# A fused gated pair of attention blocks on one core: the order of a step's matmuls written out for zero, one and two side blocks

## The chip, the core and the metric

The kernel runs on one NeuronCore of a Trainium2 chip. The metric is device time in microseconds (us) from launch to end, the median of several runs. The engines named below: TensorE (PE in the profile) multiplies and writes to PSUM; VectorE (DVE) and ScalarE (ACT) read PSUM; GpSimd (POOL) works on SBUF; SyncE (SP) issues the DMAs.

## The reference

```python
H = 32; Dh = 20                       # x: (1, 2048, 640); two weight sets, A and B
g = sigmoid((x * gate_w).sum(-1, keepdims=True))
for z in (A, B):
    q, k, v = split(x @ wqkv_z)       # per head: (2048, 20)
    p = softmax(q @ k.T * Dh ** -0.5)
    y_z = (p @ v per head, joined) @ wo_z
out = g * y_A + (1 - g) * y_B
```

Both attentions read the same x; 64 heads of dimension 20 in all, each with a 2048 x 2048 score matrix.

## The kernel before

**Tiling.** The 64 heads are taken in 16 groups of four (`g`), each group's 2048 queries in four blocks of 512 (`qb`), and each block's keys in eight pieces of 256 (`i`): 16 x 4 x 8 = 512 steps, numbered `G`. The four heads sit as two pairs (`pair`); within a pair head `j = 0` uses rows 0 to 63 of TensorE's array and `j = 1` rows 64 to 127, so two matmuls of different `j` can run side by side, and two of the same `j` come one after the other.

**What a step does on TensorE.** Eight score matmuls (`scores`, L640, 64 x 128 by 64 x 512; "e" below): each fills one PSUM bank, from which ScalarE writes an exponential (L643) into a `pt` tile. Eight matmuls for row maxima (`max_mm`, L577; "m" below): scores again, with queries and keys exchanged, 14 steps ahead of their use, each for a quarter of the 2048 keys; VectorE reduces the bank to a maximum (L588). A quarter is `ch`; the tuple `ORDER` says in which order the quarters of a unit come. For quarter 0 of `j = 0` (and of both `j` in the first group of heads) TensorE takes differences of keys of two quarters (`KD`), ScalarE writes their relu into `rl` (L581), and quarter 1's instruction on VectorE (L585) adds its own bank to it; `rl` has two buffers. Two blocks of four matmuls (`values`, L658; "V" below) weigh the previous step's exponentials with V into the one bank `acc`. They use four column strips of the array, 128 rows deep, in float32.

**Side blocks.** Projections of the next group's Q, K and V (`project_chunk`, `project_v`) and the output products (`out_tiles`, `last_tiles`) wait in the list `fill` with a first step and a due step. `slot(G)` emits one block of the one that is due first: mostly 15 full-array matmuls into one bank (L378; "X" below), copied out by ScalarE or added by VectorE. `behind(G)` says whether what is due needs more than one block in each step.

**Banks.** One of the eight PSUM banks is `acc`; the other seven serve e, m, X and the small products in turn. `take()` gives the bank that a planner's clock holds free for longest. Every engine works through its own instructions in the program's order, so a matmul whose bank is not free stops all behind it on TensorE.

**The order in a step.** The loop at the end of the program runs `q` over 0 to 7. At each `q` it emits one e, then m's that `max_step` hands out at even `q` (`j` in the order 1, 0), at `q` in `VPOS = (0, 5)` a V, and at `BLOCKS = (3, 6)` an X: at 3 if there is work, at 6 only if `behind`. So a step with one block reads, on TensorE: e m V e m e m e m X e m e m V e m e m. After the second V of the step that ends a block of queries, `take_acc` has ScalarE copy `acc` out (L743); the next V writes `acc` anew and has to wait for that copy. `advance()` after each e moves the side generators (DMAs, small vector work), eight times a step, and `todo` and `out_tasks` follow at the fourth e.

Of the kernel before, what the change touches and what calls it, by code (L numbers as in the profile page):

```python
# [31 lines left out]
NS = 8  # L32
STEPS = 2 * NG * NQ * NS
LEAD = 15
# [1 line left out]
XE = 7  # L36
QKS = 2.0 ** -12
PARTS = (0, 176, 344, 512)
BLOCKS = (3, 6)
RS = 2.0 ** 13  # L40
OB = 3
OWAIT = 20
SUM0, SUM1 = -8, 1.9
VPOS = (0, 5)
RAMP = 1.5
WEAVE = (4, 4, 3, 2)
VSTART = 14
# [3 lines left out]
T_EXP, T_MAX, T_BACK = 0.478, 0.6, 0.15  # L51
REST = 3
PRODUCT = "product"
ORDER = (0, 2, 1, 3)
LOW = -3.0e38
MS = 2.0 ** 15

# [2 lines left out]
def kernel(  # L60
# [210 lines left out]
    side = []  # L271
# [17 lines left out]
    def product():  # L289

        if parked:
            gen = parked.pop(0)
            goes = step_on(gen)
            if goes is not None:
                (side if goes else parked).append(gen)
# [256 lines left out]
    def unit_of(u):  # L552
        gq, i = divmod(u, NS)
        g, qb = divmod(gq, NQ)
        return g, qb, i
# [97 lines left out]
    def values(G, kk):  # L653
        g, qb, i = unit_of(G)
        tick_block(T_VALUES, weighed.pop((G, kk)))
        kt = 2 * i + kk
        for h in range(GH):
            nc.tensor.matmul(acc[32 * h:32 * h + VW, :], V[(g // 2) % 2][:, kt, (g % 2) * GH + h, :],  # L658
                             ptiles.pop((G, kk, h)), start=(kt == 0), stop=(kt == NT - 1))
# [296 lines left out]
    for g in range(2 * NG):  # L956
        b = g * NQ * NS
        n = g + 1
# [82 lines left out]
    def spread_of(u):  # L1041
        g, qb, i = unit_of(u)
        return {(g, qb)} if g == 0 else {(g, 0), (g, 1)}

    def max_step(G):

        ms = []
        if maxima and maxima[0][0] < G + LEAD and spread_of(maxima[0][0]) <= spread_done:
            debt[0] += 1.0 if maxima[0][0] - G >= LEAD - 1 else RAMP
            n, debt[0] = int(debt[0]), debt[0] % 1  # L1050
            for u, ch in maxima[:n]:
                ms += [lambda u=u, ch=ch, j=j: max_mm(u, ch, (j,)) for j in (1, 0)]
                if u % NS == NS - 1 and ch == ORDER[3]:
                    finishing.append(unit_of(u)[:2])
            del maxima[:n]
        return ms

    finishing = []

# [7 lines left out]
    for G in range(STEPS + 1):  # L1067
        g, qb, i = unit_of(G)
        now[0] = G
        while G < STEPS and ((g, qb) not in ready or (G and not valued(G - 1))):  # L1070
            for f in max_step(G):
                f()
            finish_step()
            advance()
            product()
            slot(G)
        for q in range(8):
            if q % 2 == 0:
                ms = max_step(G)
            n = (len(ms) + 1) // 2 if q % 2 == 0 else len(ms)  # L1080
            if G < STEPS:
                scores(G, q // 4, q // 2 % 2, (q % 2,))
            for f in ms[:n]:
                f()
            ms = ms[n:]
            if not ms:
                finish_step()
            for k in range(2):
                if q == VPOS[k]:
                    product()  # L1090
                    if G:
                        values(G - 1, k)
                        if G % NS == 0 and k == 1:
                            if G < STEPS:
                                side.append(take_acc(*unit_of(G - 1)[:2]))
                                advance()
            advance()
            if q == BLOCKS[0] or (q == BLOCKS[1] and behind(G)):
                slot(G)
            if q == 3:  # L1100
                for f in todo.pop(G, []):
                    f()
                out_tasks(G)
    end_o = take_last()
    while side or parked or fill or current or outs or last:
        advance()
# [32 lines left out]
```

## Time and profile before

| | us |
|---|---|
| median of 3 runs | 2934.09 |
| lowest, highest | 2932.76, 2935.25 |
| the profiled execution's own time | 2937.35 |
| its span, first to last instruction | 2935.5 |

The profile is of one execution. Busy times of TensorE include time in which matmuls overlap, and their ends are modelled; starts are what is read below.

### The profile page before, as it was taken

What the parts mean: (1) busy time and instruction counts of PE and PEld (TensorE: products, weight loads), DVE (VectorE), ACT (ScalarE), POOL (GpSimd) and SP (SyncE); (2) the same over time, 40 slices, a digit from 0 to 9 for tenths busy, and PEclk for the clock granted to TensorE, in tenths of its full rate; (3) what the DMA queues carried; (4) which work ended last, traced back from release to release, by engine and by line L of the source; (5) the groups of instructions that cost most, each with busy time, mean ns of one, the idle gap of its engine ahead of it and who ended that gap; (6) DMA issues with size and microseconds to landing.
All of it is one profiled execution on the core that took longest, in us unless ns stands there. A gap on an engine that the chain in (4) does not pass through costs nothing.

```text
span 2935.5 us, 63883 instructions
## 1 busy us (share of the span) xinstructions
PE 2843.9 (97%) x23474; PEld 984.7 (34%) x23474; DVE 2452.1 (84%) x4645; ACT 2539.1 (86%) x5221; POOL 655.0 (22%) x1078
## 2 busy tenths in 40 slices
PE   5999999999999999999999999999999999999998
PEld 2433323343223323234233333334433333332222
DVE  5688898878988898887988888887788888989983
ACT  2389999989988999888998989998899999988886
POOL 3221212221121212222521121222112233120010
PEclk8899999999999999999999999999999999999999
DMA  3110101101021010211112111120111212122222
GB/s 115 34 42 17 24 21 24 33 6 35 11 47 26 15 32 12 51 22 34 33 31 55 25 42 31 30 53 14 40 33 33 62 26 71 49 65 73 63 60 72
DMA packets 179839, 114.59 MB, mean 39 GB/s; under 512 B 115084, under 2 KB 153508, under 8 KB 179524
## 3 DMA queue, kind: packets, MB, share of 16 engines
q1 hardware_dynamic: 177396, 109.62, 15.2%
q8 instruction: 184, 3.01, 0.4%
q0 software_dynamic: 1472, 0.87, 0.1%
q14 instruction: 131, 1.07, 0.1%
q10 hardware_dynamic: 656, 0.00, 0.0%
HBM read 48.89 MB, written 26.61 MB: 26 GB/s over the span
## 4 chain that ended last, share of the span: by engine, by line
PE 88%; DVE 5%; ACT 2%; DMA 1%; SPq 1%; issue 1%; POOL 0%; DVEq 0%; ACTq 0%; POOLq 0%
PE acc L658 32%; PE bank L640 23%; PE bank L378 20%; PE bank L577 11%; DVE mpart L588 4%; ACT pt L643 2%; SPq L426 1%; PE bank L764 1%; PE bank L601 0%; DMA xs<-in_A_x_dram 0%; PE bank L811 0%; DVE mneg L595 0%; ACT rl L581 0%; DMA wv<-in_A_wqkv_dram 0%; PE bank L860 0%
## 5 line engine op out<-in xcount | busy, mean ns | idle before, releaser
L643 ACT ACTIVATE pt<-bank 128x512 f32<-128x512 f32 x4096 | 2225.5, 614 | 238.9 <-PE bank L577 208.3
L588 DVE TENSOR_REDUCE mpart<-bank 128x1 f32<-128x512 f32 x3040 | 1953.8, 684 | 366.7 <-PE bank L577 293.5
L640 PE MATMUL bank<-qt,kt 64*128 64x512 f16 x4096 | 1168.3, 381 | 15.5 <-DVE mpart L588 8.4
L577 PE MATMUL bank<-kt,qt 60*128 60x512 f16 x3568 | 1071.4, 381 | 16.7 <-DMA qt<-rk 6.8
L658 PE MATMUL acc<-pt,v 128*21 128x512 f32 x8192 | 1084.4, 601 | 0.5
L640 PEld LDWEIGHTS <-kt 64*128 64x128 f16 x4096 | 281.2, 94 | 1095.8 <-issue 918.5
L585 DVE CUSTOM_DVE_ANT_0 rl<-bank,rl 128x512 f32<-128x512 f32 x528 | 357.9, 681 | 7.4 <-PE bank L577 4.8
L581 ACT ACTIVATE rl<-bank 128x512 f32<-128x512 f32 x528 | 312.4, 595 | 0.0
L577 PEld LDWEIGHTS <-qt 60*128 60x128 f16 x4096 | 274.2, 94 | 95.4 <-issue 80.3
L378 PE MATMUL bank<-xx,wbh 128*128 128x168 f16 (+2 forms) x2240 | 288.6, 245 | 7.7 <-ACT pt L643 4.3
L658 PEld LDWEIGHTS acc<-pt,v 128*21 128x21 f32 x8192 | 143.0, 99 | 400.2 <-issue 363.6
L378 PE MATMUL bank<-xx,wbl 128*128 128x168 f16 (+2 forms) x1120 | 259.1, 244 | 0.0
L769 POOL CAST on<-ot 128x512 f16<-128x512 f32 x63 | 38.4, 609 | 925.7 <-DVE ot L766 905.1
L378 PEld LDWEIGHTS <-wbh 128*128 128x128 f16 x2240 | 184.4, 98 | 99.8 <-issue 92.8
L577 PE MATMUL bank<-kd,qt 60*128 60x512 f16 x528 | 202.3, 388 | 0.5 <-ACT pt L643 0.3
L378 PE MATMUL bank<-wvh,xx 128*128 128x160 f16 (+1 forms) x1280 | 159.0, 236 | 5.4 <-ACT pt L643 3.2
L378 PE MATMUL bank<-woh,o_in 128*128 128x160 f16 (+1 forms) x960 | 156.7, 256 | 4.6 <-ACT pt L643 2.8
L378 PEld LDWEIGHTS <-xx 128*128 128x128 f16 x1920 | 136.2, 98 | 58.5 <-issue 53.6
L378 PE MATMUL bank<-wvl,xx 128*128 128x160 f16 (+1 forms) x640 | 139.5, 234 | 0.0
L378 PEld LDWEIGHTS <-o_in 128*128 128x128 f16 (+1 forms) x1440 | 105.7, 97 | 73.5 <-issue 58.9
L408 POOL CAST cq<-fs 128x512 f16<-128x512 f32 x60 | 36.6, 610 | 365.5 <-ACT fs L406 365.5
L378 PE MATMUL bank<-wol,o_in 128*128 128x160 f16 (+1 forms) x480 | 115.7, 254 | 0.0
(131 smaller groups left out, 1331.6 us busy)
## 6 DMA issues: line engine op xcount, KB each, us to landing
kt<-cq SPq DMA_DIRECT2D x360, 40.0 KB
y_scr<-y_out SPq DMA_DIRECT2D x32, 320.0 KB
o_scr<-on SPq DMA_DIRECT2D x240, 40.0 KB
qt<-cq SPq DMA_DIRECT2D x180, 40.0 KB
xs<-in_A_x_dram SPq DMA_DIRECT2D x8, 640.0 KB
o_in<-o_scr SPq DMA_DIRECT2D x32, 160.0 KB
y_out<-y_scr SPq DMA_DIRECT2D x16, 320.0 KB
xx<-y_scr SPq DMA_DIRECT2D x16, 320.0 KB
```

Source lines behind the costliest of these rows:

```text
L378: nc.tensor.matmul(out_ap, a, b, start=(k == 0), stop=(k == len(pairs) - 1))
L408: nc.gpsimd.tensor_copy(hi, f)
L426: next(queues).dma_start(dst[at + 20 * k:at + 20 * k + n], src[:, part])
L577: nc.tensor.matmul(pt, QT[g % 2][r, pair, q0:q0 + P], k, start=True, stop=True)
L581: nc.scalar.activation(relus[u, j], pt, AF.Relu)
L585: nc.vector.tensor_tensor_reduce(rl, pt, rl, 1.0, LOW, OP.add, OP.max, m)
L588: nc.vector.tensor_reduce(m, pt, axis=AX.X, op=OP.max)
L640: nc.tensor.matmul(et, KT[g % 2][r, pair, kt * P:(kt + 1) * P], QT[g % 2][r, pair, qb * QB:(qb + 1) * QB], start=True, stop=True)
L643: nc.scalar.activation(pt, et, AF.Exp, scale=factor(g // 4))
L658: nc.tensor.matmul(acc[32 * h:32 * h + VW, :], V[(g // 2) % 2][:, kt, (g % 2) * GH + h, :], ptiles.pop((G, kk, h)), start=(kt == 0), stop= ...
L764: nc.tensor.matmul(pt, sel.rearrange("k h e -> k (h e)"), sr, start=True, stop=True)
L769: nc.gpsimd.tensor_copy(o[:, 0], ot)
```

## The change

`STEP` holds three written orders, for steps with no, one and two side blocks. `e0` is a score matmul of `j = 0`, `m1` a maximum's of `j = 1`, `V` a value block, `X` a side block. The number of blocks is set at the start of a step: none if nothing is waiting, two if `behind(G)`, else one. All maxima of a step are handed out at its start (`next_maxima`, the same rule as before, asked four times) and dealt to the four `m0` and four `m1`. With two blocks, one X opens the step and one closes it; with one, the X opens it. So after a step with two blocks its last X and the next step's first X stand next to each other. `ORDER` goes from (0, 2, 1, 3) to (0, 2, 3, 1). No matmul, copy or DMA is added or removed.

```diff
@@ -36,12 +36,15 @@
 XE = 7
 QKS = 2.0 ** -12
 PARTS = (0, 176, 344, 512)
-BLOCKS = (3, 6)
 RS = 2.0 ** 13
 OB = 3
 OWAIT = 20
 SUM0, SUM1 = -8, 1.9
-VPOS = (0, 5)
+
+
+STEP = ("e0 e1 m1 V e0 m1 m0 m1 e0 m0 e1 V m0 e1 e0 m1 m0 e1",
+        "X e0 m1 m0 e1 m0 m1 V m1 e0 e1 m0 e1 e0 V m0 e1 e0 m1",
+        "X m0 m1 e0 m1 e0 e1 V e1 e0 m1 m0 V e1 m0 m1 m0 e0 e1 X")
 RAMP = 1.5
 WEAVE = (4, 4, 3, 2)
 VSTART = 14
@@ -51,7 +54,7 @@
 T_EXP, T_MAX, T_BACK = 0.478, 0.6, 0.15
 REST = 3
 PRODUCT = "product"
-ORDER = (0, 2, 1, 3)
+ORDER = (0, 2, 3, 1)
 LOW = -3.0e38
 MS = 2.0 ** 15
 
@@ -1042,18 +1045,25 @@
         g, qb, i = unit_of(u)
         return {(g, qb)} if g == 0 else {(g, 0), (g, 1)}
 
-    def max_step(G):
-
-        ms = []
-        if maxima and maxima[0][0] < G + LEAD and spread_of(maxima[0][0]) <= spread_done:
-            debt[0] += 1.0 if maxima[0][0] - G >= LEAD - 1 else RAMP
-            n, debt[0] = int(debt[0]), debt[0] % 1
-            for u, ch in maxima[:n]:
-                ms += [lambda u=u, ch=ch, j=j: max_mm(u, ch, (j,)) for j in (1, 0)]
-                if u % NS == NS - 1 and ch == ORDER[3]:
-                    finishing.append(unit_of(u)[:2])
-            del maxima[:n]
-        return ms
+    def next_maxima(G, n):
+
+        some = []
+        for _ in range(n):
+            if maxima and maxima[0][0] < G + LEAD and spread_of(maxima[0][0]) <= spread_done:
+                debt[0] += 1.0 if maxima[0][0] - G >= LEAD - 1 else RAMP
+                n, debt[0] = int(debt[0]), debt[0] % 1
+                some += maxima[:n]
+                del maxima[:n]
+        return some
+
+    half_done = set()
+
+    def one_max(u, ch, j):
+        max_mm(u, ch, (j,))
+        if u % NS == NS - 1 and ch == ORDER[3]:
+            if unit_of(u)[:2] in half_done:
+                finishing.append(unit_of(u)[:2])
+            half_done.add(unit_of(u)[:2])
 
     finishing = []
 
@@ -1068,39 +1078,41 @@
         g, qb, i = unit_of(G)
         now[0] = G
         while G < STEPS and ((g, qb) not in ready or (G and not valued(G - 1))):
-            for f in max_step(G):
-                f()
+            for u, ch in next_maxima(G, 1):
+                for j in (1, 0):
+                    one_max(u, ch, j)
             finish_step()
             advance()
             product()
             slot(G)
-        for q in range(8):
-            if q % 2 == 0:
-                ms = max_step(G)
-            n = (len(ms) + 1) // 2 if q % 2 == 0 else len(ms)
-            if G < STEPS:
-                scores(G, q // 4, q // 2 % 2, (q % 2,))
-            for f in ms[:n]:
-                f()
-            ms = ms[n:]
-            if not ms:
+        some = next_maxima(G, 4)
+        blocks = 0 if not current and not any(f[0] <= G for f in fill) else 2 if behind(G) else 1
+        count = {}
+        for what in STEP[blocks].split():
+            k = count[what] = count.get(what, 0) + 1
+            if what[0] == "e":
+                q = sum(count.get(f"e{j}", 0) for j in range(2)) - 1
+                j = int(what[1])
+                if G < STEPS:
+                    scores(G, (k - 1) // 2, (k - 1) % 2, (j,))
                 finish_step()
-            for k in range(2):
-                if q == VPOS[k]:
-                    product()
-                    if G:
-                        values(G - 1, k)
-                        if G % NS == 0 and k == 1:
-                            if G < STEPS:
-                                side.append(take_acc(*unit_of(G - 1)[:2]))
-                                advance()
-            advance()
-            if q == BLOCKS[0] or (q == BLOCKS[1] and behind(G)):
+                advance()
+                if q == 3:
+                    for f in todo.pop(G, []):
+                        f()
+                    out_tasks(G)
+            elif what[0] == "m":
+                for u, ch in some[(k - 1) * len(some) // 4:k * len(some) // 4]:
+                    one_max(u, ch, int(what[1]))
+            elif what == "V":
+                product()
+                if G:
+                    values(G - 1, k - 1)
+                    if G % NS == 0 and k == 2 and G < STEPS:
+                        side.append(take_acc(*unit_of(G - 1)[:2]))
+                        advance()
+            else:
                 slot(G)
-            if q == 3:
-                for f in todo.pop(G, []):
-                    f()
-                out_tasks(G)
     end_o = take_last()
     while side or parked or fill or current or outs or last:
         advance()
```

TensorE, in step 347, one with two blocks. In the rows, `acc` and `v1` belong to a V, L640 is an e, L577 an m and L378 an X. Before, the last of a V's four matmuls, one e, one m, and the start of the step's second X:

```order
L658 MATMUL acc_90<-pt_25841,v1_87 21x512
L640 LDWEIGHTS kt0_82
L640 MATMUL bank5_96<-qt0_80,kt0_82 128x512
L577 LDWEIGHTS qt1_81
L577 MATMUL bank0_91<-kt1_83,qt1_81 128x512
L378 LDWEIGHTS wbh_25395
L378 MATMUL bank3_94<-xx_79,wbh_25395 128x168
```

Now, at the end of the corresponding step (lines are three higher: L381 is X):

```order
L381 LDWEIGHTS wbh_25413
L381 MATMUL bank2_93<-xx_79,wbh_25413 128x168
L381 LDWEIGHTS wbl_25414
L381 MATMUL bank2_93<-xx_79,wbl_25414 128x168
L381 LDWEIGHTS wbh_25180
L381 MATMUL bank3_94<-xx_79,wbh_25180 128x176
L381 LDWEIGHTS wbh_25180
L381 MATMUL bank3_94<-xx_79,wbh_25180 128x176
```

The block into bank 2 is followed by the next one, into bank 3, with no e or m between them; the short stretch of two score matmuls is gone.

ScalarE, around step 184, the first of a new block of queries, with one side block. L643 is an exponential, L581 the relu, L406 the copy of an X, L743 the copy of `acc`. Before:

```order
L581 ACTIVATE rl<-bank_92 128x512
L643 ACTIVATE pt<-bank_95 128x512
L643 ACTIVATE pt<-bank_97 128x512
L406 ACTIVATE fs<-bank_91 128x176
L643 ACTIVATE pt<-bank_94 128x512
L643 ACTIVATE pt<-bank_92 128x512
L743 ACTIVATE ot<-acc 128x512
L643 ACTIVATE pt<-bank_97 128x512
L643 ACTIVATE pt<-bank_96 128x512
L643 ACTIVATE pt<-bank_92 128x512
```

Now (L646, L584, L409 and L746 are the same lines):

```order
L409 ACTIVATE fs<-bank_92 128x176
L646 ACTIVATE pt<-bank_94 128x512
L584 ACTIVATE rl<-bank_96 128x512
L646 ACTIVATE pt<-bank_95 128x512
L646 ACTIVATE pt<-bank_91 128x512
L646 ACTIVATE pt<-bank_96 128x512
L646 ACTIVATE pt<-bank_95 128x512
L646 ACTIVATE pt<-bank_93 128x512
L746 ACTIVATE ot<-acc 128x512
L646 ACTIVATE pt<-bank_94 128x512
L646 ACTIVATE pt<-bank_96 128x512
L409 ACTIVATE fs<-bank_95 128x168
```

The copy of the side block moved from two exponentials ahead of the copy of `acc` to the front of the step, and four exponentials of one stretch now stand directly ahead of the copy of `acc`, where two stood.

## Rows read from the trace of the kernel before

**Rows 1.** The page: span, and busy time of TensorE with its share.

```profile
span 2935.5 us, 63883 instructions
PE 2843.9 (97%) x23474; PEld 984.7 (34%) x23474; DVE 2452.1 (84%) x4645; ACT 2539.1 (86%) x5221; POOL 655.0 (22%) x1078
```

**Rows 2.** Stretches from:to; their us, then each engine's busy us and instructions, clock, DMA.

```profile
1143.86:1164.80 20.94, 20.94 (x190) 7.54 (x188) 18.00 (x33) 19.30 (x41) 7.62 (x10) 1.00 0.10 24
1069.95:1083.77 13.82, 13.74 (x100) 3.23 (x96) 13.14 (x24) 13.55 (x28) 0.00 (x0) 1.00 0.12 25
1326.86:1346.53 19.67, 19.67 (x190) 8.87 (x186) 13.81 (x25) 15.66 (x34) 9.39 (x12) 1.00 0.03 6
137.56:176.68 39.12, 38.75 (x338) 16.96 (x336) 32.32 (x78) 30.84 (x67) 10.55 (x12) 1.00 0.12 27
...
1121.75:1138.59 16.84, 16.47 (x145) 6.10 (x143) 14.09 (x26) 15.23 (x34) 3.26 (x5) 1.00 0.06 12
```

**Rows 3.** Timeline of TensorE, one-block step: start, us, engine, line, tiles, count.

```profile
1144.17 1.06 PE L658 MATMUL acc<-pt,v 128*21 128x512 f32 x8
1145.16 0.39 PE L640 MATMUL bank<-qt,kt 64*128 64x512 f16 x1
...
1145.92 0.32 PE L378 MATMUL bank<-xx,wbh 128*128 128x168 f16 x2
...
1146.94 0.24 PE L378 MATMUL bank<-xx,wbl 128*128 128x168 f16 x1
1147.11 0.39 PE L640 MATMUL bank<-qt,kt 64*128 64x512 f16 x1
...
1147.65 1.05 PE L658 MATMUL acc<-pt,v 128*21 128x512 f32 x8
```

**Rows 4.** Timeline of TensorE, two-block step: the stretch before the second block.

```profile
1331.64 0.39 PE L640 MATMUL bank<-qt,kt 64*128 64x512 f16 x1
...
1331.96 0.33 PE L378 MATMUL bank<-xx,wbh 128*128 128x176 f16 x2
```

**Rows 5.** Timeline of TensorE before the first step: side blocks one after another.

```profile
123.37 0.30 PE L378 MATMUL bank<-wvh,xx 128*128 128x161 f16 x2
123.51 0.23 PE L378 MATMUL bank<-wvl,xx 128*128 128x161 f16 x1
123.58 0.31 PE L378 MATMUL bank<-wvh,xx 128*128 128x161 f16 x2
```

**Rows 6.** Timeline of ScalarE where a block of queries ends; [idle before].

```profile
1125.59 1.14 ACT L643 ACTIVATE pt<-bank 128x512 f32<-128x512 f32 x2
1127.08 0.60 ACT L743 ACTIVATE ot<-acc 128x512 f32<-128x512 f32 x1 [0.36 <-issue]
```

**Rows 7.** Timeline of TensorE at the same place; [idle before <- who ended it].

```profile
1125.59 0.39 PE L764 MATMUL bank<-sr,sel 8*128 8x512 f16 x1
1125.90 1.06 PE L658 MATMUL acc<-pt,v 128*21 128x512 f32 x8
1126.89 0.39 PE L640 MATMUL bank<-qt,kt 64*128 64x512 f16 x1
...
1127.73 1.06 PE L658 MATMUL acc<-pt,v 128*21 128x512 f32 x8
...
1129.80 0.31 PE L378 MATMUL bank<-xx,wbh 128*128 128x168 f16 x2 [0.20 <-ACT pt L643]
```

**Rows 8.** The copy of acc in the whole run: count, duration min/median/max in ns.

```profile
L743 ACT ACTIVATE ot<-acc x63: 597/597/645, 195.0 to 2881.7; 128x512 f32<-128x512 f32 x63
```

**Rows 9.** Timeline of VectorE in a step without a block.

```profile
1069.97 3.87 DVE L588 TENSOR_REDUCE mpart<-bank 128x1 f32<-128x512 f32 x6
1073.76 0.68 DVE L585 CUSTOM_DVE_ANT_0 rl<-bank,rl 128x512 f32<-128x512 f32 x1
1074.36 0.08 DVE L585 DVE_READ_ACCUMULATOR2_ANT mpart<- 128x1 f32 x1
1074.58 0.69 DVE L588 TENSOR_REDUCE mpart<-bank 128x1 f32<-128x512 f32 x1
```

## The prediction

> **What bounds the kernel now.** First the page: TensorE counts as busy for 97% of the span [rows 1]. Its ends are modelled, so this does not yet say that it is the bound. For that I read stretches that begin and end at a step's first score matmul [rows 2], by the number of side blocks in a step. One block: 20.94 us for four steps, 5.24 each, with ScalarE busy 92% and VectorE 86%. Two blocks: 19.67 us for three, 6.56 each, ScalarE at 80%, VectorE at 70%. No block: 13.82 us for three, 4.61 each, VectorE at 95% and ScalarE at 98%.
>
> Next the timeline of TensorE in a step with one block [rows 3]. A V takes 0.99 us from its start to the next start, a stretch of six score and maximum matmuls 0.76, of four 0.54 (1147.11 to 1147.65), an X of 168 columns 1.19. Two V, two stretches of six, one of four and the X make 1.98 + 1.52 + 0.54 + 1.19 = 5.23, which is the whole step. So a step with one block has no wait in it; TensorE's own instructions are its length. Stretches of two, four and six take 0.32 [rows 4], 0.54 and 0.76: 0.22 for a pair of matmuls that run side by side, and 0.10 once per stretch, for changing from one shape of the array to another.
>
> A step without a block needs two V and eight pairs in two stretches, 1.98 + 1.76 + 0.20 = 3.94, but takes 4.61. There VectorE sets the time: six reductions, the sum with its read, and the next reduction follow each other from 1069.97 to 1074.58, 4.61 us, with 0.14 idle [rows 9]; ScalarE's 98% leaves no room either.
>
> At the end of a block of queries ScalarE sits idle for 0.36 us until the last V is done, and then copies `acc` for 0.60 [rows 6]. The next V starts 0.84 after the stretch ahead of it (0.76 usually), and the X after that waits 0.20 for a bank from ScalarE [rows 7]. The three steps there take 16.84 us [rows 2] against 15.71 for three ordinary ones: 1.13 more, 0.31 of it a small extra product [rows 7], the rest another small one and waits.
>
> **The change part by part.** The counts are taken from the order of TensorE's instructions: before, 97 steps have no block, 353 one, 62 two; after, 105, 337 and 70.
>
> *Touching blocks.* After a step with two blocks, its last X and the next step's first X stand side by side; that happens 69 times. Before, the second X cut a stretch of six into two and four. Gone are one stretch (0.32 + 0.54 against 0.76, 0.10) and one change around an X. What a change around X costs: within a block the matmuls start every 1.02/14 = 0.073 us, and from its last to the next score matmul it is 0.17 [rows 3], so 0.10. That two X in a row don't pay this is seen ahead of the first step, where they follow each other at 0.21 for three matmuls, also across the border at 123.44 [rows 5]. So 0.20 for each of the 62 steps that had two blocks already: -12.4 us. It would be half if the second X waited for its bank: -6.
>
> *Eight more pairs of steps with two blocks and none, in place of one and one*, because `behind` is now asked ahead of the step's first block: (6.56 - 0.20 + 4.61) - 2 x 5.24 = +0.49 each, +4 us (0 to 5).
>
> *Steps with one block.* The same stretches, 6, 6 and 4, with the same two V and one X, now in the order X 6 V 6 V 4: the six changes remain. The new order alternates `j` strictly, the old one paired neighbours; both give the same three, three and two pairs. Nothing, if the seven banks come free in time. What hides the risk is the 8% that ScalarE and 14% that VectorE have left [rows 2]. The exponentials are dealt as 2, 4, 2 in the three stretches, with the relu in the first, against 3, 3, 2 before with the relu in the second: nine items for ScalarE in both cases, four of them in the same stretch as before. 0 taken, 0 to +17 (0.05 in each of 337 steps) kept for the range.
>
> *Steps without a block.* Their order has nine pairs instead of eight: one stretch begins and ends on the same half of the array. 3.94 + 0.22 = 4.16 is still under VectorE's 4.61, which hides it: 0. If that cover were gone, +0.22 for each of 105.
>
> *The copy of `acc`.* Before, one stretch of six (0.76) lies between the last V and the next; now a stretch of four, X and a stretch of six, 0.54 + 1.19 + 0.76 = 2.49. So V no longer waits. On ScalarE four exponentials of a stretch stand ahead of the copy instead of two, enough to fill the time until V is done: the 0.36 of idling goes. But the copy's 0.60 stays, and comes when ScalarE has most queued; what was a wait of the next-but-one X becomes a wait of the next step's first stretch. Of 63 copies [rows 8] about 45 stand in steps with one block. Per copy the gain lies between 0 and 0.36 (the idle time), at most 0.8 (all of the excess but the extra product). I take 0.15, since the X's wait of 0.20 is the part nearest to the idle time: -7 us (0 to -16).
>
> *The first group of heads.* There both `j` have a relu, and six quarters a step are handed out for some twelve steps. Tokens `m0` and `m1` then hold two matmuls of the same half, in seven two-block steps: 12 pairs against 10, +0.43 each, +3 us. And quarter 1 is now last, so its sum on VectorE stands directly ahead of the next unit's relu, which needs its buffer of `rl`. In those steps ScalarE is busy for 30.84 of 39.12 us and VectorE for 32.32 [rows 2], so most of that wait lies in idle time: +2 (0 to +12).
>
> *Side blocks' own traffic.* A block moves by at most half a step. With it move its copy on ScalarE, the casts on GpSimd (22% busy, [rows 1]) and, at least ten `advance` later, the DMAs on SyncE's queue; the number of `advance` in a step is the same. 0. After the last step two side blocks more are left over: +1.
>
> Sum: -12.4 + 4 - 7 + 3 + 2 + 1 = -9.4 us. Against the profiled execution 2937.35 - 9.4 = 2927.9; that execution lay 3.3 over the median, so against the median 2934.09: **2925**.
>
> **The rivals.**
>
> *Banks run short in one-block steps (slower).* Four exponentials in one stretch of six, behind a relu and the copy of a side block, could make TensorE wait for ScalarE once in each step. That such waits happen is seen at the copy of `acc`, 0.20 [rows 7]; for it speaks ScalarE's 92%. Against it: every stretch still brings ScalarE at most four items, as before. At 0.05 in 337 steps: 2925 + 17 = 2942, slower. The gain is gone from 0.028 a step.
>
> *The end of a block of queries comes free (faster).* If the lead of 2.49 us takes in the copy altogether, the excess over the two extra products goes, some 0.6 of the 1.13: -27 instead of -7: 2905. Against it: ScalarE has the same work, and 8% of 5.24 us is 0.4 a step to make up for 0.60.
>
> *Touching blocks give nothing.* Two X are 2.3 us in which VectorE and ScalarE get nothing new, and the work left out comes in a rush afterwards; or the second X waits, so that the change doesn't do what it says. Then -12.4 falls away: 2937, no change. For it: VectorE already is the bound where there is no block [rows 9]. Against: it has 30% to spare in two-block steps [rows 2]. The Trainium skill, "TensorEngine Tiling (Array Packing)", PSUM Bottleneck, says that tiling speeds up TensorE but not the emptying of PSUM, which may become the bottleneck; by that rule the freed time is lost and this rival holds. The trace bears it out in steps without a block and not in those with two, so it moves this chance little.
>
> **How the numbers follow.** My forecast (2916 to 2934) has 0.5, short banks 0.17, the free end 0.18, no gain from touching 0.15. About 0.2% (6 us) is what a measurement of this kernel can tell from no change: 2928.2 to 2940. Faster: three quarters of the forecast and the free end, 0.38 + 0.18 = 0.56. Same: 0.12 and most of the last rival, with a little of the first, 0.28. Slower: 0.16. The range takes in the free end and one-block waits of 0.05 with some of the ramp's bound: 2904 to 2945.
>
> **What would show it.** Steps with two blocks at 6.3 to 6.4 us, X following X at the same spacing as inside a block; steps with one block at 5.2 and with none at 4.6. The idle time ahead of the copy of `acc` gone, and V after it without a wait. It is wrong if one-block steps are over 5.24, with TensorE waiting for exponentials ahead of a score matmul, or if the first 230 us grow by over 10 us.

## The result and the profile after

| | before | after |
|---|---|---|
| median, us | 2934.09 | 2945.99 |
| lowest, highest | 2932.04, 2935.25 | 2943.58, 2948.75 |
| the profiled execution's own time | 2937.35 | 2943.85 |

After is slower by 0.4%: ratio 1.004, 95% interval 1.0029 to 1.0051. The two profiled executions lie 6.5 us apart, the medians 11.9: the mean granted clock of TensorE was 0.991 in the profile of before and 0.994 in that of after (with levels of one half and one, some 53 and 35 us at the lower), and the profile of after is of the execution with the highest clock of its five, so the profiles show less than the whole difference. In the code of after, lines stand 3 lower than in before (L640 is L643, L577 is L580, L378 is L381, L743 is L746).

The page of after (answers to [rows 1]):

```profile
span 2942.0 us, 63335 instructions
PE 2825.4 (96%) x23474; PEld 978.4 (33%) x23474; DVE 2429.7 (83%) x4645; ACT 2560.1 (87%) x5221; POOL 655.0 (22%) x1078
```

TensorE's busy time has fallen by 18.5 us while the span has grown by 6.5: it stands idle for 25 us more. The stretches (answers to [rows 2], same columns): four steps with one block, three with none, three with two, a step without a block in which a small product stands, and the three steps behind the end of a block of queries.

```profile
1502.70:1523.64 20.94, 20.94 (x189) 7.54 (x188) 17.53 (x33) 19.60 (x40) 8.46 (x13) 1.00 0.11 26
1426.59:1440.52 13.93, 13.54 (x99) 3.15 (x97) 13.20 (x26) 13.85 (x28) 8.47 (x8) 1.00 0.23 51
1337.92:1356.94 19.02, 19.02 (x188) 8.97 (x186) 13.57 (x25) 15.65 (x34) 9.37 (x12) 1.00 0.03 5
1415.61:1422.02 6.41, 5.15 (x36) 1.17 (x34) 4.60 (x10) 4.78 (x11) 4.88 (x8) 1.00 0.29 60
...
1137.66:1154.09 16.43, 16.43 (x145) 5.86 (x145) 14.38 (x28) 15.37 (x33) 4.05 (x7) 1.00 0.06 12
```

One-block steps: 5.24, as before. Two-block steps: 6.34, for 6.56. Steps without a block: 4.64, for 4.61. The end of a block of queries: 16.43, for 16.84. Four of the five are as forecast or a little better. The fourth line is what was not: 6.41 for a step of the same kind as the 4.64 ones, in which a small product stands. Of the steps without a block that no side block borders on, those with a small product take 5.12 us in before and 6.15 in after (medians of 29 and 27).

Where TensorE waits, in the view of waits (engine, tile, line, whom it waited for; us in total, times, longest). First before, then after, the rows that differ most:

```profile
PE bank L378 <- ACT pt L643: 10.2, 47, 0.3
...
PE bank L378 <- DVE mpart L588: 6.6, 42, 0.3
...
PE bank L601 <- DVE mneg L595: 1.3, 1, 1.3
PE bank L180 <- DVE dg L173: 1.2, 1, 1.2
```

```profile
PE bank L604 <- DVE mneg L598: 11.4, 11, 2.0
PE bank L183 <- DVE dg L176: 9.1, 9, 1.4
...
PE bank L166 <- DVE m L227: 6.6, 5, 1.3
...
PE bank L166 <- DVE m L269: 1.2, 2, 0.6
```

Gone are nearly all waits of X (L378) for ScalarE's exponentials and VectorE's reductions to free a bank, 16.8 us in 89 pieces (2.2 in 2 are left). New are waits of three kinds of small product, 28 us for 3: the transposition of the row maxima (L604, waits for VectorE's `mneg`), the two products of the scales (L166 on `m`, L183 on `dg`). One of them, on TensorE's timeline of after and then on VectorE's:

```profile
380.02 0.38 PE L580 MATMUL bank<-kt,qt 60*128 60x512 f16 x1
381.43 0.27 PE L604 MATMUL bank<-ident,mneg 128*16 128x128 f32 x1 [1.03 <-DVE mneg L598]
381.62 1.06 PE L661 MATMUL acc<-pt,v 128*21 128x512 f32 x8
```

```profile
377.13 3.21 DVE L591 TENSOR_REDUCE mpart<-bank 128x1 f32<-128x512 f32 x5 [0.37 <-PE bank L580]
380.26 0.68 DVE L588 CUSTOM_DVE_ANT_0 rl<-bank,rl 128x512 f32<-128x512 f32 x1
...
381.06 0.22 DVE L598 TENSOR_REDUCE mneg<-mpart 128x16 f32<-128x64 f32 x1
```

TensorE has run through its stretch at 380.4 and has the transposition next. VectorE had five reductions (until 380.34) and a sum (until 380.94) ahead of `mneg`, and is done with it at 381.3. The V behind the transposition, which needs none of this, waits with it.

### The profile page after: what moved, and what is told of

Read it like the earlier page. It is cut to its first block, busy times and chain, and to the rows that moved or that the text cites. A ratio compares the mean times of both kernels' runs of the same rounds, so it can differ in the third digit from the quotient of the medians.

```text
span 2942.0 us, 63335 instructions
## 1 busy us (share of the span) xinstructions
PE 2825.4 (96%) x23474; PEld 978.4 (33%) x23474; DVE 2429.7 (83%) x4645; ACT 2560.1 (87%) x5221; POOL 655.0 (22%) x1078
## 3 DMA queue, kind: packets, MB, share of 16 engines
q14 instruction: 126, 1.03, 0.1%
## 4 chain that ended last, share of the span: by engine, by line
PE 81%; ACT 6%; DVE 5%; SPq 3%; issue 3%; DMA 2%; POOL 0%; DVEq 0%; ACTq 0%; POOLq 0%
PE acc L661 30%; PE bank L381 18%; PE bank L643 16%; PE bank L580 15%; ACT pt L646 5%; SPq L429 3%; DVE mpart L591 3%; DVE rl L588 1%; ACT rl L584 1%; PE bank L767 1%; PE bank L604 0%; DMA xs<-in_A_x_dram 0%; DMA wv<-in_A_wqkv_dram 0%; PE bank L814 0%; ACT ot L746 0%
## 5 line engine op out<-in xcount | busy, mean ns | idle before, releaser
L646 ACT ACTIVATE pt<-bank 128x512 f32<-128x512 f32 x4096 | 2185.9, 612 | 188.6 <-PE bank L643 114.8
L643 PE MATMUL bank<-qt,kt 64*128 64x512 f16 x4096 | 1051.3, 381 | 19.0 <-DVE mpart L591 4.2
L580 PE MATMUL bank<-kt,qt 60*128 60x512 f16 x3568 | 1022.3, 381 | 20.9 <-DMA qt<-rk 6.8
L580 PEld LDWEIGHTS <-qt 60*128 60x128 f16 x4096 | 229.2, 94 | 818.5 <-issue 741.4
L643 PEld LDWEIGHTS <-kt 64*128 64x128 f16 x4096 | 246.2, 94 | 358.6 <-issue 233.4
L584 ACT ACTIVATE rl<-bank 128x512 f32<-128x512 f32 x528 | 316.3, 602 | 14.3 <-PE bank L580 6.2
L381 PE MATMUL bank<-xx,wbh 128*128 128x168 f16 (+2 forms) x2240 | 284.1, 244 | 3.8 <-ACT wbh L308 2.4
L381 PE MATMUL bank<-xx,wbl 128*128 128x168 f16 (+2 forms) x1120 | 258.0, 243 | 0.5 <-POOL mpart L572 0.5
L381 PEld LDWEIGHTS <-wbh 128*128 128x128 f16 x2240 | 183.1, 98 | 88.3 <-issue 81.3
L580 PE MATMUL bank<-kd,qt 60*128 60x512 f16 x528 | 196.7, 379 | 0.9 <-ACT pt L646 0.7
L381 PE MATMUL bank<-wvh,xx 128*128 128x160 f16 (+1 forms) x1280 | 157.5, 235 | 2.7 <-DVE mpart L591 2.2
L381 PE MATMUL bank<-woh,o_in 128*128 128x160 f16 (+1 forms) x960 | 155.3, 256 | 0.6 <-ACT mt L609 0.4
L381 PEld LDWEIGHTS <-xx 128*128 128x128 f16 x1920 | 133.1, 98 | 55.8 <-issue 53.1
L381 PE MATMUL bank<-wvl,xx 128*128 128x160 f16 (+1 forms) x640 | 138.3, 233 | 0.0
L612 POOL CAST m4r<-mt 16x128 f16<-16x128 f32 x128 | 33.1, 282 | 452.6 <-ACT mt L609 452.6
L381 PEld LDWEIGHTS <-o_in 128*128 128x128 f16 (+1 forms) x1440 | 104.0, 97 | 69.8 <-issue 55.1
L756 POOL TENSOR_SCALAR sq<-sq 128x16 f32<-128x16 f32 x63 | 16.0, 254 | 457.6 <-DVE sq L754 430.3
```

What stands on the lines that cost most here:

```text
L381: nc.tensor.matmul(out_ap, a, b, start=(k == 0), stop=(k == len(pairs) - 1))
L580: nc.tensor.matmul(pt, QT[g % 2][r, pair, q0:q0 + P], k, start=True, stop=True)
L584: nc.scalar.activation(relus[u, j], pt, AF.Relu)
L612: nc.gpsimd.tensor_copy(m4[:, k, :], mt)
L643: nc.tensor.matmul(et, KT[g % 2][r, pair, kt * P:(kt + 1) * P], QT[g % 2][r, pair, qb * QB:(qb + 1) * QB], start=True, stop=True)
L646: nc.scalar.activation(pt, et, AF.Exp, scale=factor(g // 4))
```

## The experiments

Before was run again beside each set of kernels on the same chip: medians 2934.76, 2934.3, 2933.9 and 2933.42 for the four sets below, 2933.2 for the last two kernels. Ratios are against these. Where two kernels of different sets are compared by their medians below, up to 1.6 us can be the set's.

**One part of the change undone or eased at a time.** `a_later`: after, with the generators of the small products waiting four more `advance` in the main loop, at three places, of which one is shown (lines then stand 5 to 9 lower still). It is the edit "later" below.

```diff
+    def more():
+        return range(4 if now[0] >= 0 else 0)
...
         for _ in range(REST):
             yield
+        for _ in more():
+            yield
         yield PRODUCT
```

> The changed kernel (2946), with the small products of the side generators (the transpose of the maxima, L604; the transpose and the broadcast of the scales, L166 and L183) asked for four score matmuls later in the main loop. Theory A (the written orders put four score matmuls, and with them four moves of the generators, into one stretch, so a small product reaches a value block before VectorE has made its input): the waits of these products on VectorE, 28 us in the trace of the changed kernel against 4 before, fall under 8, and the time to 2920 to 2930. Rival B (the odd pair in steps without a block, and the waits are only where VectorE's lag shows): the waits move to other instructions, 2940 to 2948. Rival C (a sum on VectorE directly ahead of the next unit's relu holds ScalarE): 2940 to 2948.

Measured 2937.29, ratio 1.0008 (0.9999 to 1.0017): 8.7 us less than after. The waits did what theory A says, the time fell by a third to a half of what it says. Its waits:

```profile
PE bank L613 <- DVE mneg L605: 1.3, 1, 1.3
PE bank L190 <- DVE dg L181: 1.2, 1, 1.2
```

The waits on `m` are gone, the other two as short as in before, and the same place on TensorE's timeline has no wait (the transposition now mostly stands one step later):

```profile
389.55 0.38 PE L587 MATMUL bank<-kt,qt 60*128 60x512 f16 x1
389.85 0.28 PE L613 MATMUL bank<-ident,mneg 128*16 128x128 f32 x1
```

So 26 us of waits went and the time fell by 9. Part of the rest is seen in the traces: at three places where VectorE waits for weights (told below) TensorE now waits 6.0, 5.5 and 4.2 us, for 4.2, 4.9 and 2.0 in after, and the mean granted clock is 0.988, for 0.994.

`a_quarters`: after with the old order of quarters.

```diff
-ORDER = (0, 2, 3, 1)
+ORDER = (0, 2, 1, 3)
```

> The changed kernel with the quarters in the old order 0, 2, 1, 3. Theory A: within 3 us of the changed kernel, 2943 to 2949. Rival B: the same. Rival C: back by most of the difference, 2932 to 2938, the first group of heads (128 to 330 us) shorter by 3 to 8.

Measured 2945.29, ratio 1.0037 (1.0023 to 1.005): by itself it gives nothing, as theories A and B say; rival C falls.

`a_zero`: after with the old order of a step without a block.

```diff
-STEP = ("e0 e1 m1 V e0 m1 m0 m1 e0 m0 e1 V m0 e1 e0 m1 m0 e1",
+STEP = ("e0 m1 V e1 m0 e0 m1 e1 m0 e0 m1 e1 m0 V e0 m1 e1 m0",
```

> The changed kernel with the old order in steps without a block (105 steps), the written orders in the others. Theory A: these steps hold eight of the eleven waits of the maxima's transpose, 1.1 us each beyond VectorE's own pace, so -9 us for them and 0.04 a step for the odd pair, -4: 2932 to 2938. Rival B: all of the difference, 2928 to 2936, with the waits of the scales' products (17 us) gone as well. Rival C: 2946.

Measured 2939.02, ratio 1.0012 (1.0003 to 1.0021): 7 us less than after, 1 us short of theory A; rival B falls, since the waits of the scales' products stay. The waits on `mneg` fall to 2.9 us, those on `dg` to 6.7, and those on `m` (6.6) stay: the new order of this step makes the first kind. What is left of the others stands, in the trace, in steps with one block, ahead of their second V.

`a_apart`: after with the old order of a step with two blocks.

```diff
-        "X m0 m1 e0 m1 e0 e1 V e1 e0 m1 m0 V e1 m0 m1 m0 e0 e1 X")
+        "e0 m1 V e1 m0 e0 m1 e1 m0 X e0 m1 e1 m0 V e0 m1 X e1 m0")
```

> The changed kernel with the old order in the 70 steps with two blocks, so that blocks no longer touch behind such a step. What touching is worth: steps with two blocks go from 6.34 back to 6.57, 70 x 0.22 = 15 us: 2961 (2956 to 2966), if nothing else hangs on that order. If touching gives nothing in the sum, 2946.

Measured 2952.27, ratio 1.0057 (1.0044 to 1.0071): 6.3 more than after, so the order with touching blocks does gain, but less than half of the 15 expected. TensorE's timeline of after, where the second X begins at 1342.87:

```profile
1342.64 0.32 PE L381 MATMUL bank<-xx,wbh 128*128 128x176 f16 x2
1342.79 0.24 PE L381 MATMUL bank<-xx,wbl 128*128 128x176 f16 x1
1342.87 0.31 PE L381 MATMUL bank<-xx,wbh 128*128 128x168 f16 x2
1343.01 0.24 PE L381 MATMUL bank<-xx,wbl 128*128 128x168 f16 x1
```

0.08 from the last matmul of one block to the first of the next, as inside a block.

**Parts put together.** `a_later_q` is "later" with the old order of quarters, `a_best` this with the old order of a step without a block as well, `a_allold` is after with all three old orders and the old order of quarters (so only its new machinery is left), and `b_sooner` is before with `REST = 0` for 3.

> After, with the small products of the side blocks four `advance` later in the main loop, and with the quarters of keys in the old order 0, 2, 1, 3. The later products alone gave 2937.3. Theory (what the later products leave over sits in the first group of heads, where the new order of quarters needs two halves at once): 4 to 5 us less than that, 2931 to 2934, and group 0 at 196 to 199 us for 204. Rival (the order of quarters costs nothing, as it did by itself): 2936 to 2939.

Measured 2932.05, ratio 0.9991 (0.9982 to 1.0), as the theory has it. The order of quarters costs 5.2 us, once the waits for small products are away; in the traces the first group of heads takes 204.3 us in `a_later` and 196.9 here.

> After, with later products, the old order of quarters, and the old order of the steps without a block; what is left of the change is the order of one-block and two-block steps, with blocks that touch. If the gains of these two orders and the losses of the other parts add up: 0.4 us less in each of some 45 ends of a query block in one-block steps (-15), 0.2 in each of some 60 pairs of touching blocks less the pairs that the change adds (-8), the first group of heads +0 to +5: 2915 to 2927. Rival (TensorE's work is only shifted between groups, and half-clock stretches take back what the order gives): 2930 to 2938.

Measured 2928.05, ratio 0.9977 (0.9968 to 0.9986): faster than before by 6 us, between the theory's 7 to 19 and the rival, so neither held.

> After's new machinery, with all three old orders of a step and the old order of the quarters: what is left of the change is how maxima are dealt out and where `advance` and the finishing stand. Theory (the loss comes from the orders, through the count of `advance` ahead of a value block): within 3 us of before, 2931 to 2937, and waits of TensorE on `mneg`, `dg` and `m` of 2 to 8 us in all as in before. Rival (the new machinery costs by itself): 2940 or more.

Measured 2943.44, ratio 1.0029 (1.0017 to 1.004). The theory fell: with every order old, 9 of the 12 us are still there, and its waits on `mneg` and `dg` are 2.0 and 1.1 us.

> Before, with no `advance` between VectorE's input and the small product of the scales and of the selections (REST 0 for 3). Theory (how many `advance` stand between the two decides whether TensorE waits): the waits on `dg`, `mneg` and `m` rise from 3 us to 15 to 40, and the time by 5 to 25 us, 2939 to 2959, with no order of a step changed. Rival (the products come only at a value block, and three calls more or less change which one seldom): within 3 us of before.

Measured 3019.87, ratio 1.0291 (1.0277 to 1.0305), far past the theory's bound of 25 us:

```profile
PE bank L601 <- DVE mneg L595: 96.0, 64, 2.4
```

Three calls of `advance` fewer make each of the 64 transpositions wait 1.5 us, in the order of before. The theory had the other small products wait as well; their waits did not rise (1.2 us on `dg`, none on `m`).

**Orders and distances crossed.** `b_later` is before with "later", `a_allold_later` is `a_allold` with it, `a_best_o` is `a_best` with the old order of a step with one block, `a_best8` is `a_best` with eight more `advance` for four.

> Before, with the small products four `advance` later in the main loop and nothing else changed. Theory (before hardly waited for them: 3 us on `dg`, `mneg` and `m` in all): within 3 us of before, 2931 to 2937, so what a_best gains over before is the orders' own. Rival (the later products gain by themselves, orders or not): 2924 to 2930, and then the orders give nothing.

Measured 2938.32, ratio 1.0017 (1.0008 to 1.0026): the later products by themselves cost before 4 us, a little more than the theory allowed; they are no gain of their own, so the rival falls.

> a_allold (after's machinery, every order old: 2943.4) with the small products four `advance` later. Theory (the machinery's 9 us come from its `advance`, which now stands ahead of the maxima and of the value block and not behind them, so that products come one value block early): 2931 to 2937. Rival (they come from how the maxima are dealt out): 2941 to 2945, and waits on `dg`, `mneg` and `m` that were already 3 us don't matter.

Measured 2960.85, ratio 1.0093 (1.0078 to 1.0109): both theories fell; it grew by 17.4. X's waits for ScalarE are more than doubled:

```profile
PE bank L388 <- ACT pt L655: 20.8, 89, 0.3
```

(`a_allold`: 8.3 in 40; for VectorE 6.3 us in both.) The traces of the two show where. "Later" moves the transposition of the maxima from the third to the fourth step of a block of queries, in all 61 blocks of the main part, and in 49 of them X of the fourth step now waits, 12.4 us in all. One of them:

```profile
462.08 0.28 PE L613 MATMUL bank<-ident,mneg 128*16 128x128 f32 x1
...
464.35 0.31 PE L388 MATMUL bank<-xx,wbh 128*128 128x176 f16 x2 [0.25 <-ACT pt L655]
```

In this block the third step goes from 5.64 us in `a_allold` to 5.43 and the fourth from 5.27 to 5.78: 0.30 more, which over 49 to 61 blocks gives 15 to 18 us, an estimate that takes in the 17.4. In `b_later` the transposition moves just so and X does not wait (9.9 us in 46 in all; the fourth step takes 5.48). There ScalarE's copy of the transposition stands ahead of the exponentials of the stretch, here behind the first of them; that this is why was not tried.

> a_best (2928.05) with the old order of a step with one block: of the change only the order of two-block steps is left, with touching blocks behind them. Theory (the one-block order frees TensorE from the copy of `acc` at some 45 ends of a query block, 0.35 to 0.4 us each, 16 to 18): 2941 to 2947. Rival (that wait comes back as a wait for a bank in the same query block): 2926 to 2932.

Measured 2948.54, ratio 1.0049 (1.0036 to 1.0063): among the other parts of `a_best` the new one-block order is worth 20.5 us, a little over the theory's 13 to 19. In `a_best_o` X waits 20.6 us in 89 pieces for ScalarE and 6.2 in 39 for VectorE; in `a_best`:

```profile
PE bank L388 <- ACT pt L655: 1.5, 6, 0.2
...
PE bank L388 <- DVE mpart L598: 0.2, 1, 0.2
```

That is 25 us of waits. Only some 7 us of them stand in the second step of a block of queries, behind the copy of `acc` of which the theory speaks; 10.3 us stand in the fourth step, where "later" had made them, and 5.8 are VectorE's in the third.

> a_best with the small products eight `advance` later in place of four. Theory (four already take the waits away, what is left of them being 2 to 3 us): 2925 to 2931. Rival (the chain of the scales gets longer, and work that hangs on it runs out: waits for `m`, `rk` or `wbh`): 2933 to 2945.

Measured 2929.99, ratio 0.9984 (0.9975 to 0.9993), as the theory has it: four are enough.

**The machinery, and waits that all versions share.** `a_allold_adv` and `after_adv` collect `finish_step`, `advance` and the step's tasks, and carry them out ahead of the next e or X, where before has them, in place of right behind the e. The lines that carry them out are left out here.

```diff
-                finish_step()
-                advance()
-                if q == 3:
-                    for f in todo.pop(G, []):
-                        f()
-                    out_tasks(G)
+                behind_it.append(q)
```

> a_allold (after's machinery, every order old: 2943.4) with the call that ends a maximum, `advance` and the step's own tasks put back behind the maxima, the value block and the side block that follow a score, where before has them. Theory (the machinery costs 9 us because every side block gets its `advance` one value block sooner, so that its products land one value block sooner than where the old order had room for them): 2932 to 2937. Rival (the 9 us come from how the maxima are dealt out, all of a step's at its start): 2940 to 2946.

Measured 2939.54, ratio 1.002 (1.0011 to 1.0029): between the two. Each against before of its own set, 6.1 of the 9.1 us stay, and 3.0 come from the place of `advance` (3.9 between the two medians as they stand).

> After itself (2946) with the same three things put back behind, all new orders kept. Theory (the distance between VectorE's input and the small product, counted in `advance`, decides): the waits of TensorE on `mneg`, `dg` and `m` fall from 28 us to 5 to 18 and the time to 2936 to 2943. Rival (one `advance` is too little for the value block that follows four scores): waits of 22 us or more, 2943 to 2948.

Measured 2947.17, ratio 1.0046 (1.0032 to 1.006): the rival. Waits on `mneg` and `dg` are still 11.1 and 10.9 us, only those on `m` are gone; one call is too little.

Last, a wait that before has as well: VectorE for weights (`wstage`) from memory. Here are, of `a_best`, a row of VectorE's waits, then TensorE's and SyncE's timelines at one of three such places:

```profile
DVE wmax L234 <- DMA wstage<-in_B_wqkv_dram: 14.6, 2, 8.0
```

```profile
871.61 1.06 PE L670 MATMUL acc<-pt,v 128*21 128x512 f32 x8
872.60 0.39 PE L652 MATMUL bank<-qt,kt 64*128 64x512 f16 x1
879.88 0.58 PE L587 MATMUL bank<-kt,qt 60*128 60x512 f16 x1 [6.90 <-DVE mpart L598]
...
881.60 1.91 PE L670 MATMUL acc<-pt,v 128*21 128x512 f32 x8
```

```profile
866.25 3.66 SPq L436 DMA_DIRECT2D qt<-cq  x5
869.95 2.26 SPq L436 DMA_DIRECT2D qt<-rk  x3
872.26 2.22 SPq L436 DMA_DIRECT2D kt<-cq  x3
874.58 0.42 SPq L240 DMA_DIRECT2D wstage<-in_B_wqkv_dram  x1
```

SyncE works off a long row of copies into `qt` and `kt` at about 0.74 us each and comes to the load at 874.58. VectorE's next instruction from 870.6 on is the reduction of that weight, which starts at 878.6; all reductions of maxima behind it wait, and TensorE has no bank. How long this lasts depends on when a kernel comes there and on when SyncE gets to the load: VectorE of before comes 2.4 us later, its load is issued at 872.91, and it waits 3.7 us. `a_best_sp` and `b_sp` are `a_best` and before with the loads and reductions further apart, or later; `after_sp` and `a_later_q_sp` are after and `a_later_q` with the same edit.

```diff
-                    tasks(b + 2, 2, parts)
+                    tasks(b + 2, 3, parts)
...
-        tasks(b + 8, 1, parts)
+        tasks(b + 12, 1, parts)
```

> a_best (2928.05) with the reads of the next weights' maxima later: three steps apart for two, and in the two layers' output weights from step 12 of a group for 8. In a_best VectorE stands 8.0 and 6.7 us for `wstage` from memory and 4.4 us for GpSimd's product on it, its queue behind it and TensorE with it (20 us in all); SyncE issued the loads late, behind the copies into `kt` and `qt` at 0.74 us each. Theory (these three waits take back what TensorE gains ahead of them): they go, 2908 to 2918. Rival (the weights come as late with the next load, or the later scale products are awaited): 2924 to 2932.

Measured 2902.66, ratio 0.9898 (0.9883 to 0.9914): the fastest of all, 25 us below `a_best`, where the theory had 10 to 20. No wait of VectorE for `wstage` is left in its trace.

> Before with the same later reads. Before waits 5.6, 5.9 and 5.0 us at these three places. Theory: 2919 to 2926. Rival (what is gained there is lost at the next such wait): 2931 to 2936.

Measured 2914.97, ratio 0.9937 (0.9924 to 0.9951): 18 us without any change of an order, more than the theory's 8 to 15.

> After (2946) with the later reads of the weights of b_sp and a_best_sp, nothing else. After waits 4.4, 2.0 and 6.1 us at the three places (12.5), before 5.6, 5.9 and 5.0 (16.5), and b_sp gained 18. Theory (a kernel that comes late to the three places waits less there, so they hid some of the change's loss): 2931 to 2936, that is 16 to 21 us over b_sp's 2915.0 where after is 12 over before. Rival (the waits are the same for both, the loss is 12 with or without them): 2926 to 2930.

Measured 2929.56, ratio 0.9987 (0.9978 to 0.9996): within the rival's bounds, near the upper. Without these waits the change costs 14.6 us (against `b_sp`) in place of 11.9, as if they had hidden about 3; in the traces VectorE waits there for 13.4 us in before and 12.1 in after, so 1.3 of it is seen. (The sums of the expectation, 16.5 and 12.5, are not those of the traces.)

> a_best_sp (2902.7) with the new order of a step without a block, in other words a_later_q with the later reads. Theory (that order costs more than the 4 us between a_later_q and a_best, because a_best lost part of its lead in the three waits, 20 us there for 17): 2908 to 2913. Rival (4 us, with or without the waits): 2905.5 to 2907.5.

Measured 2907.62, ratio 0.9914 (0.9901 to 0.9928): between the two. The order of a step without a block costs 5.0 us against `a_best_sp`. From `after_sp` the later products and the quarters together give 21.9, for the 13.9 from after to `a_later_q`, so the waits for weights had hidden 8 us of what `a_later_q` gains.

## Why the prediction was wrong

It said 2925 and a gain of 9.4 us on the profile; it came out at 2946, a loss, just past the upper end of the range. Step by step, in us of the medians; each row is one kernel's median less another's, so it holds beside the parts that the two share, and may differ beside others:

| step of the prediction | forecast | measured | from |
|---|---|---|---|
| touching blocks | -12.4 | -12.3 | `a_best_o` against `a_allold_later` |
| eight more pairs, and the tail (with the maxima dealt out at a step's start) | +5 | +6.1 | `a_allold_adv` against before |
| place of `advance`, old orders | 0 | +3.9 | `a_allold` against `a_allold_adv` |
| one-block order with the copy of `acc` | -7 | -20.5 | `a_best` against `a_best_o` |
| order of steps without a block | 0 | +4.0 | `a_later_q` against `a_best` |
| quarters, first group | +5 | +5.2 | `a_later` against `a_later_q` |
| small products come too early | 0 | +8.7 | after against `a_later` |
| the longer distance, old orders | none | +17.4 | `a_allold_later` against `a_allold` |

The rows lead from before over `a_allold_adv`, `a_allold`, `a_allold_later`, `a_best_o`, `a_best`, `a_later_q` and `a_later` to after, so that their sum, +12.5, is by construction after less before of the fourth set (+11.9 in after's own set); it tests nothing.

*The failed step is "Side blocks' own traffic": "the number of `advance` in a step is the same. 0."* The number is the same; what counts is how much time lies between the calls. Ahead of the transposition of the maxima and of the product on `dg` a generator lets `REST` = 3 calls pass behind VectorE's input, ahead of the product on `m` fewer, and then the product goes out at the next V. In the old one-block order three or five e lie between two V, the five spread over 2.5 us with X among them; in the new one it is four both times, and four of them (`m1 e0 e1 m0 e1 e0`) within one stretch of 0.76 us. In the step without a block, three e follow on its last m0 (its e1, and e0 e1 of the next step) before the next V, where the old order has one e ahead of that V and lets the product go out one V later; eight of the eleven waits on `mneg`, 1.03 us each, stand there. So the three calls can pass in under 0.76 us, while VectorE can have some 3 us of reductions ahead in its queue. The rows on `mneg`, `dg` and `m` show the wait: 28.3 us, 25.8 more than before, against 14.6 of X's waits that the change took away. `a_later` shows that these waits go with distance alone, and that 8.7 us of the time go with them. `b_sooner` shows the same for the transposition in the old order.

*It is not the distance alone, but order and distance together.* Medians; all four have the change's machinery, and "orders" takes in that of the quarters:

| | three calls | seven calls |
|---|---|---|
| old orders (`a_allold`, `a_allold_later`) | 2943.4 | 2960.9 |
| new orders (after, `a_later`) | 2946.0 | 2937.3 |

At seven calls the orders of the change are worth 23.6 us, at three they cost 2.6. The distance of three suited the order that it stood in. Why the old order loses 17 at seven is seen in the fourth step of a block of queries, where the transposition then stands and X waits (12.4 us); why X does not wait for it in `b_later` was not tried, and neither was where the 4 us of `b_later` sit.

*Touching blocks.* Right in mechanism: 0.08 at the border, two-block steps at 6.34 for the 6.36 that the working gives. That the sum agrees to 0.1 us is in part luck: the 12.4 are for 62 steps, the two kernels have some 70, for which the working gives 14, and in after itself the order is worth 6.3 (`a_apart`), half as much. The rule of the Trainium skill that the prediction set against it ("TensorEngine Tiling (Array Packing)", PSUM Bottleneck) did not decide here: VectorE is busy 13.57 of 19.02 us in these steps and TensorE all of them.

*The copy of `acc`.* Right in mechanism, and too small for what came with it. ScalarE's idle time ahead of the copy, before and after:

```profile
its engine sat idle before it (us, times) until:
  issue: 9.6, 31
  PE acc L658: 2.8, 14
who waited for it (us, times):
  PEld acc L658: 26.5, 54
```

```profile
its engine sat idle before it (us, times) until:
  issue: 1.2, 6
  PE acc L661: 0.5, 3
who waited for it (us, times):
  PEld acc L661: 2.7, 4
```

The gain was taken as 0.15 for each of 45 copies; the three steps went from 16.84 to 16.43, 0.41: in turn 5.59, 5.61 and 5.64 to 5.55, 5.40 and 5.48. X waits for ScalarE in the second of them [rows 7] and for VectorE in the third, which the prediction did not count:

```profile
1135.23 0.30 PE L378 MATMUL bank<-xx,wbh 128*128 128x168 f16 x2 [0.15 <-DVE mpart L588]
```

Of the 89 waits of X in the run, 39 (8.0 us) stand in second steps and 41 (6.4 us) in third ones, so the part with the copy, 8 us, is near the 7 forecast, and the other is one that it left out. 45 times 0.41 is 18.5, an estimate near the 20.5 of the table, but in the 20.5 are 10 us of waits that "later" had made. The rival of the free end, 0.6 a copy, lies past the 0.41 of the two together; the rival of banks short in one-block steps did not come, 5.24 as before.

*Steps without a block* are 4.64 where nothing else stands in them, for 4.60 to 4.61 in before: VectorE covers the ninth pair but for 0.04, as said. What the prediction left out are those in which a small product stands. In after their order costs 7.0 us (`a_zero`), with 8.5 of waits on `mneg`. With the later products these waits are gone and 4.0 to 5.0 us remain; in the traces of `a_best` and `a_later_q` there are 90 such steps that no side block borders on: the 33 with a small product go from 171.8 to 176.2 us in all, the other 57 from 266.3 to 264.4.

*The first group* is +5.2 by the quarters, as forecast, but only once the other waits are gone; in after itself undoing them gives 0.7, though the first group is shorter there too (200.8 to 195.9 us in the traces): what was gained in it was lost behind it.

## What to carry to other kernels

When an order is rewritten, list everything whose distance is counted in calls or steps of the old one (rests, due times, reads of a load), and turn each count into us in the new one; what the call count hides, a wait view by tile shows at once. Change the order and these distances together, since each may look like a loss alone. And look for waits on a queue that runs at its own pace before judging any gain upstream of it: here three waits for weights that came late by SyncE's queue were worth 18 us in before, more than the change.

## What had not been expected of the hardware

A DMA issue in a row of them held SyncE's queue for 0.74 us (3.66 for five, 2.22 for three), so that a load placed in the program at step 134 was issued at 874.58, in step 136, and VectorE began on it 4.0 us later. The pause cost more than its own length. Stretches of `a_best` before, in and behind it, then of `a_best_sp` (columns as in [rows 2]):

```profile
862.00:872.00 10.00, 9.83 (x69) 2.27 (x70) 8.27 (x16) 9.78 (x20) 1.74 (x2) 1.00 0.16 33
872.00:882.00 10.00, 3.10 (x18) 0.47 (x14) 3.42 (x8) 2.88 (x6) 0.00 (x0) 0.61 0.38 91
882.00:892.00 10.00, 9.88 (x73) 2.60 (x65) 8.67 (x17) 7.24 (x16) 1.82 (x3) 0.88 0.25 65
```

```profile
872.00:882.00 10.00, 9.70 (x88) 3.36 (x81) 9.12 (x18) 9.56 (x21) 1.21 (x2) 1.00 0.36 83
```

The granted clock, a mean of TensorE's two levels, was 0.61 in the ten us of the pause, in which TensorE had stood still for 6.90, and 0.88 in the next ten; the V at 881.60 took 1.91 us, where 1.06 is usual. In `a_best_sp`, which has no pause there, it stays at 1.00. This is likely why `b_sp` gained 18 us where VectorE had waited for 13.4 in before (3.7, 5.9 and 3.9): the mean granted clock is 0.995 in its profile, for 0.991, some 24 us less at the lower level. The surplus was not measured by itself.
